# A chunked-attention and softplus-FFN kernel: the first product of six of its nine token tiles by Strassen's seven products

## The chip, the core and the metric

The kernel runs on one core of a Trainium2 chip. The core has a matrix engine (TensorE, in the profile PE, with its weight loads as PEld), a vector engine (VectorE, DVE), a scalar engine (ScalarE, ACT), GpSimd (POOL), a queue engine (SyncE, SP) and sixteen DMA engines. Each engine takes its instructions in the order of the program and waits on semaphores. The metric is the device time of one execution in microseconds; less is better. Three runs before the change took 861.62 to 861.96 us, with a median of 861.85 us.

## The reference

Attention within chunks of 64 tokens (8 batches, 8 heads, 576 tokens, head size 64), then a feed-forward layer with softplus on 4608 tokens, all in float32:

```python
scores = scale * np.matmul(q_c, k_c.transpose(0, 1, 2, 4, 3))
scores = scores - np.max(scores, axis=-1, keepdims=True)
attn = np.exp(scores)
attn = attn / (np.sum(attn, axis=-1, keepdims=True) + 1e-09)
x = np.matmul(attn, v_c)            # as 4608 x 512
h = x @ w_in                        # 512 x 2048
g = np.maximum(h, 0.0) + np.log1p(np.exp(-np.abs(h)))
out = g @ w_out                     # 2048 x 512
```

## The kernel before

**Tiles.** The 4608 tokens are nine m-tiles of 512 (`m`, four blocks of 128 tokens each, 36 blocks in all); the 2048 columns of `w_in` are 16 strips of 128 (`fc`). Each number is split into a high part rounded to `float32r` and the low rest, and each product is three matmuls: high by high, low by high, high by low. For one `m` and `fc` (number g = 16 m + fc) the first product G1 is 12 matmuls of 128x128 by 128x512 (four slices of K, three terms), from `gemm1` (L587). ACT then makes u = softplus (L595) and its high part `g_hi` (L599), DVE or POOL the low part `g_lo` (L603), and the second product G2 adds 12 matmuls (four tiles of 128 tokens, three terms, L621) into four PSUM banks `po`, which ACT and DVE evacuate (`ev`, L630) after the 16th strip. The tiles `g_hi` and `g_lo` have two buffers, u has one, and `pa`, PSUM for G1 and attention, has two tiles of two banks.

**Stages.** First some 30 us of attention for the first m-tile; then m-tile 0, beside which the weights are loaded and split ("decode", POOL and ACT, to about 120 us); then m-tiles 1 to 8, for which everything stands in SBUF.

**Attention** goes on beside the FFN in 17 *bursts* (`burst`, L462 and L550): a burst is the scores of one pair of blocks and the value product of the pair before. Around it ACT copies the result to x (L562) and does the exponentials (`exp`, L525, with a table load each way), DVE the maxima (L507), the subtraction (L512), the denominators (L530 to L532), the norm (L537) and transposes (L439, L474 and, for three blocks, L486); SP loads q, k, v in DMAs of 32 or 64 KB and swaps quarters of the transposed scores by DMA (`eT<-ka`).

**Order.** A planner (`class Plan`) is given every task with its engine, cost, needs, buffers and urgency, and its list schedule, made while the program is built, fixes the order of instructions on each engine; nothing is reordered at run time. The order of PE is given by the list `seq`: G1 of g, then G2 of g - 1, with bursts after given G1. DMAs of SP and ACT take eight semaphores in turn, so that a DMA also waits for the one eight places before it in the program, whichever of the two queues that is on.

Of the kernel before, what the change touches and what calls it, by code (L numbers as in the profile page):

```python
# [33 lines left out]
class Plan:  # L34
# [14 lines left out]
    def add(  # L49
        self, name, eng, cost, fn, needs=(), urg=0.0, table=None, take=(), kb=0, slack=0.0, after=(), port=False, parts=1,  # L50
        late={}
# [3 lines left out]
            take=take, kb=kb, slack=slack, seq=len(self.tasks), port=port or eng == "POOL", parts=parts, late=late,  # L55
        )

    def order(self):
# [23 lines left out]
        def has_room(t, now):  # L82
            for pool, _ in t["take"]:
                cap, used = self.pools[pool]
                if len(used) >= cap:
                    for n in used[len(used) - cap]:
                        if n not in fin or fin[n] + self.CROSS > now:
                            return False
            return True
# [59 lines left out]
def chunked_attention_softplus_ffn(  # L149
# [54 lines left out]
    wi = [tuple(const.tile([P, KC, half], F32R, name=n) for n in ("wi_hi", "wi_lo"))]  # L204
    stage = [later.tile([P, KC * half], F32, name="wib") for _ in range(2)]
# [4 lines left out]
    early = [xpool.tile([P, TPM, DM], F32, name="x") for _ in range(2)]  # L210
    xs = []

    def x_of(m):
        while len(xs) <= min(m, 1):
            xs.append([xpool.tile([P, 2 * TPM, KC, C], F32R, name="x") for _ in range(2)])
        return xs[m % 2]
# [6 lines left out]
    tops = [const.tile([P, UW], I32, name=f"top{j}") for j in range(TOP_BUFS)]  # L223
    for t in tops:
        nc.vector.memset(t, 0)
    live = {}

    def raw_tile():
        return ld.tile([P, 2 * UW + 16], I32, name="raw", bufs=RAW_BUFS)
# [4 lines left out]
    def w_load(u, is_in, fc):  # L234
        queue = nc.gpsimd if u in LOAD_POOL else nc.sync
        raw = raw_tile()
# [17 lines left out]
    def w_low(u):  # L254
        if u < STAGED:
            o = u * UW
            low = stage[o // (KC * half)][:, o % (KC * half) :][:, :UW].bitcast(I32)
        else:
            low = ld.tile([P, UW], I32, name="low", bufs=LOW_BUFS)
# [7 lines left out]

    def w_parts(u, is_in, fc):
        t = live["low", u].bitcast(F32)
        if is_in:  # L270
            if fc // HALF_FC == len(wi):
                wi.append(tuple(later.tile([P, KC, half], F32R, name="wib") for _ in range(2)))
# [655 lines left out]
```

## Time and profile before

| | before |
|---|---|
| median of three runs | 861.85 us |
| span of the profiled execution, first to last instruction | 859.1 us |
| PE busy | 847.1 us, 99% |
| DVE, ACT, POOL busy | 346.8, 314.0, 75.1 us |
| DMA | 63.13 MB, mean 73 GB/s |

The profile gives the profiled execution's own time as its span of 859.1 us; the median of the runs is 2.75 us above it, which lies before the first and after the last instruction. In the groups a row is line, engine, operation, tiles, count, then busy time and mean duration, then the idle time before it and what ended it. In a timeline a row is start (us), duration (us), engine, line, operation. "xN" is a count of instructions. Busy times of PE overlap a little: a 128x512 matmul is shown with 389 ns, while the next one starts earlier.

### The profile page before, as it was taken

The numbers are of one execution on the slowest core, as the hardware profiler recorded it, in microseconds if no ns is written. First come the engines' busy times: TensorE is split into PE (matmuls) and PEld (weight loads), VectorE is DVE, ScalarE is ACT, GpSimd is POOL, SyncE is SP. The second block draws the span as 40 slices with busy tenths as digits, with TensorE's granted clock in tenths as the row PEclk, the third lists the DMA queues.
The fourth block names the chain that finished last, engine by engine and source line by source line (L and its number), as shares of the span: only waits on it lengthen the run. The fifth ranks groups of instructions, "written<-read, shape, count | busy, mean of one in ns | idle before, by whom it ended". The sixth has DMA issues, their size and how long they took to land.

```text
span 859.1 us, 14819 instructions
## 1 busy us (share of the span) xinstructions
PE 847.1 (99%) x5889; PEld 700.6 (82%) x5889; DVE 346.8 (40%) x600; ACT 314.0 (37%) x493; POOL 75.1 (9%) x76
## 2 busy tenths in 40 slices
PE   8899999999999999999999999999999999999997
PEld 7687888888888888888888888888888888888886
DVE  4999865333433251515252333424342514121111
ACT  4857744322424242424242423324242324222222
POOL 1576751000000000000000000000000000000000
PEclk9999999999999999999999999999999999999999
DMA  9987733222232224232323223222312241010001
GB/s 225 237 213 188 222 92 94 47 46 50 43 98 42 50 43 102 41 58 36 87 54 60 39 53 96 42 52 41 98 41 53 42 103 37 13 50 0 1 1 49
DMA packets 207061, 63.13 MB, mean 73 GB/s; under 512 B 184592, under 2 KB 200464, under 8 KB 206992
## 3 DMA queue, kind: packets, MB, share of 16 engines
q1 hardware_dynamic: 206848, 62.06, 31.6%
q8 instruction: 46, 0.75, 0.4%
q14 instruction: 23, 0.19, 0.1%
q10 hardware_dynamic: 144, 0.13, 0.0%
HBM read 45.09 MB, written 9.44 MB: 63 GB/s over the span
## 4 chain that ended last, share of the span: by engine, by line
PE 90%; DVE 3%; DMA 2%; SPq 1%; ACT 1%; issue 1%; POOL 0%; DVEq 0%; POOLq 0%; ACTq 0%
PE po L621 43%; PE pa L587 42%; PE pa L550 2%; DMA raw<-in_moe_w_in_dram 2%; PE pa L462 2%; SPq L318 1%; DMA raw<-in_moe_w_out_dram 1%; DVE wib L266 1%; DVE qe L449 1%; DVE ka L449 1%; DVE g_lo L603 0%; DVE eT L486 0%; ACT u L595 0%; ACT wib L261 0%; ACT top L252 0%
## 5 line engine op out<-in xcount | busy, mean ns | idle before, releaser
L603 DVE TENSOR_TENSOR g_lo<-u,g_hi 128x512 fp32r<-128x512 f32 (+1 forms) x133 | 92.5, 696 | 441.8 <-ACT g_hi L599 441.6
L595 ACT ACTIVATE u<-pa 128x512 f32<-128x512 f32 (+1 forms) x146 | 86.4, 592 | 503.6 <-PE pa L587 496.3
L587 PE MATMUL pa<-x,wib 128*128 128x512 f32 x864 | 207.5, 389 | 0.0
L587 PEld LDWEIGHTS pa<-x,wib 128*128 128x128 f32 x864 | 162.2, 188 | 33.7
L587 PE MATMUL pa<-x,wi_hi 128*128 128x512 f32 (+1 forms) x592 | 186.1, 383 | 0.0
L621 PE MATMUL po<-late,g_hi 128*128 128x512 f32 x539 | 166.2, 391 | 0.1
L587 PEld LDWEIGHTS pa<-x,wi_hi 128*128 128x128 f32 x592 | 109.6, 188 | 22.0
L621 PEld LDWEIGHTS po<-late,g_hi 128*128 128x128 f32 x539 | 100.5, 188 | 21.6 <-POOL late L291 0.5
L621 PE MATMUL po<-wo_hi,g_hi 128*128 128x512 f32 x288 | 109.5, 393 | 0.0
L621 PE MATMUL po<-wo_lo,g_hi 128*128 128x512 f32 x288 | 108.7, 390 | 0.6 <-POOL wo_lo L291 0.6
L621 PE MATMUL po<-wo_hi,g_lo 128*128 128x512 f32 x288 | 108.7, 390 | 0.0
L587 PE MATMUL pa<-x,wi_lo 128*128 128x512 f32 (+1 forms) x296 | 108.6, 383 | 0.0
L621 PE MATMUL po<-late,g_lo 128*128 128x512 f32 x287 | 107.8, 389 | 0.0
L599 ACT CAST g_hi<-u 128x512 fp32r<-128x512 f32 (+1 forms) x146 | 89.7, 615 | 4.4
L621 PEld LDWEIGHTS po<-wo_lo,g_hi 128*128 128x128 f32 x288 | 54.0, 188 | 12.1 <-POOL wo_lo L291 1.0
L587 PEld LDWEIGHTS pa<-x,wi_lo 128*128 128x128 f32 x296 | 54.7, 188 | 10.9
L621 PEld LDWEIGHTS po<-wo_hi,g_lo 128*128 128x128 f32 x288 | 54.0, 188 | 11.5 <-DVE g_lo L603 0.3
L621 PEld LDWEIGHTS po<-late,g_lo 128*128 128x128 f32 x287 | 53.9, 188 | 11.3
L621 PEld LDWEIGHTS po<-wo_hi,g_hi 128*128 128x128 f32 x288 | 53.7, 188 | 11.2
L530 DVE TENSOR_REDUCE den<-qe 128x8 f32<-128x512 f32 x32 | 21.1, 661 | 23.2 <-ACT qe L525 23.2
L566 DVE TENSOR_TENSOR x<-pa,x 128x512 fp32r<-128x512 f32 x36 | 24.5, 682 | 1.8 <-ACT x L562 1.8
L439 DVE STREAM_TRANSPOSE ka<-k 128x512 f32<-128x512 f32 x28 | 19.8, 706 | 13.3 <-DMA eT<-ka 13.3
(114 smaller groups left out, 581.9 us busy)
## 6 DMA issues: line engine op xcount, KB each, us to landing
out_dram<-raw SPq DMA_DIRECT2D x35, 256.0 KB, 2.4
raw<-in_moe_w_in_dram SPq DMA_DIRECT2D x16, 512.0 KB, 5.2
raw<-in_moe_w_out_dram SPq DMA_DIRECT2D x16, 512.0 KB, 4.6
eT<-ka SPq DMA_DIRECT2D x232, 32.0 KB, 1.9
q<-in_q_dram SPq DMA_DIRECT2D x224, 32.0 KB, 2.1
k<-in_k_dram SPq DMA_DIRECT2D x224, 32.0 KB, 2.1
q<-in_v_dram SPq DMA_DIRECT2D x60, 64.0 KB, 2.4
k<-in_v_dram SPq DMA_DIRECT2D x60, 64.0 KB, 2.4
```

What stands on the lines that cost most here:

```text
L266: nc.vector.tensor_tensor(low, low, live.pop(("top", u)), op=ALU.add)
L439: nc.vector.transpose(t, live.pop((n, i)))
L449: nc.vector.transpose(dst[d : d + BL, :, tb], src[s : s + BL, :, dh])
L462: nc.tensor.matmul(pa[o, c2, col : col + C], qT[r, a * HP + hl, :], kT[r, a * HP + hl, :], start=True, stop=True,)
L530: nc.vector.tensor_reduce(den, e, axis=AX.X, op=ALU.add)
L550: nc.tensor.matmul(pa[o, a, col : col + C], vt[r, 4 * j + 2 * h2 + c2, :], eT[r, :, 4 * c2 + 2 * j + h2, :], start=True, stop=True,)
L566: nc.vector.tensor_tensor(lo, live.pop(("xp", i)), hi.bitcast(F32), op=ALU.subtract)
L587: nc.tensor.matmul(ph, wt[:, c, fs], x[:, ts_, c, :], start=(n == 0), stop=(n == 3 * KC - 1))
L595: nc.scalar.activation(w["u"], w["ph"], AF.Softplus)
L599: nc.scalar.copy(w["hi"], w["u"])
L603: (nc.gpsimd if pool else nc.vector).tensor_tensor(w["lo"], w["u"], w["hi"].bitcast(F32), op=ALU.subtract)
L621: nc.tensor.matmul(pos[w["m"]][t], terms[n][0][:, j * P : (j + 1) * P], terms[n][1], start=(w["first"] and n == 0), stop=n == 2 and (w["la ...
```

## The change

**What it does.** `FAST = 3`: m-tiles 0 to 2 stay as they are. M-tiles 3 to 8 are taken in three *supers* of two m-tiles (1024 tokens). Within a super, two strips `fc` at a time (a *pair*, eight per super), the product of 2x2 blocks (two m-tiles; two strips; two halves of K) is formed by seven products P0 to P6 instead of eight. Each product is six matmuls (two slices of K, three terms), so a pair has 42 where it had 48; there are 24 pairs. P4, P5, P6 accumulate on the banks of P1, P2, P0, after ACT has copied what these held (`hold`: s0, s1, s2); POOL (`d`, `e`) and DVE (`c22`, `f`, `f2`, `c11`) then combine them (`mix`).

**Weight sums.** The seven weight operands of each pair are formed once during m-tiles 1 and 2 (`w_total`, `w_sums`, `w_sum_lo` on POOL: per pair two operations of 128x512, five of 128x256, then two of 128x512 and one of 128x256; `w_sum_hi` and the stores on ACT: 48 stores of sums and 12 of unchanged blocks), and written to DRAM (`scratch`, 1.75 MB a pair). In each super the operands of each pair come back in two loads on ACT's queue (`ring_load`: 1 MB for P0 to P3, free after P3 of the pair before; 0.75 MB for P4 to P6, free after P6).

**Sums of x.** Before each super five sums of blocks of x (`x_sum`, k = 2 and 4 on POOL), and seven splits into high (`x_hi`, ACT) and low (`x_lo`, DVE), all 128x1024.

**Half of u in DRAM.** The pairs yield u for both m-tiles; that of the second goes to DRAM (`spill_store`, 512 KB a pair) and comes back (`spill_load`) in the super's second phase, in which the 16 G2 of the second m-tile follow one another without a G1. In the first phase PE does P0 to P6 of a pair (six matmuls each), then the two G2 of the pair before.

**Attention.** Bursts move: nine of the seventeen stand in m-tiles 0 to 2 (after G1 4, 8, 15, 21, 26, 31, 35, 40, 44), four each in supers 0 and 1 (after pairs 2, 5, 7 and after the ninth G2 of the second phase). From block 9 on the swaps by DMA become DVE transposes (eight of 32x256 per block), and the norms of blocks 10 to 19 go to POOL.

The core of the diff:

```diff
-    later = ctx.enter_context(tc.tile_pool(name="later", bufs=2))
+    FAST = 3
+    HC = MT // 2
+
+    later = ctx.enter_context(tc.tile_pool(name="later", bufs=4))
     late = ctx.enter_context(tc.tile_pool(name="late", bufs=LATE))
     const = ctx.enter_context(tc.tile_pool(name="const", bufs=1))
-    xpool = ctx.enter_context(tc.tile_pool(name="xpool", bufs=4))
+    xpool = ctx.enter_context(tc.tile_pool(name="xpool", bufs=2))
+    dram = ctx.enter_context(tc.tile_pool(name="dram", bufs=1, space=bass.MemoryType.DRAM))
...
+    def high(n):
+        if "high" not in live:
+            live["high"] = [later.tile([P, 4 * MT], F32R if j < 3 else F32, name="wib") for j in (0, 1, 2, 3)]
+        return live["high"][n]
+
+    def x_image(k):
+        if k < NX:
+            return [t.rearrange("p a k f -> p (a k f)")[:, 2 * MT * k : 2 * MT * (k + 1)] for t in wi[0]]
+        return high(k - NX)[:, : 2 * MT], high(k - NX)[:, 2 * MT :]
...
+    def w_image(w, k):
+        if w["name"] == "0_0" and k < NX:
+            return raw_tile(1 + k // 2).bitcast(F32R)[:, k % 2 * MT : (k % 2 + 1) * MT]
+        t = x_of(FAST - 1)[k // NX].rearrange("p s k t -> p (s k t)")
+        return t[:, k % NX * MT : (k % NX + 1) * MT]
...
+    def w_total(j, n):
+        if n == 0:
+            live["wt", j] = raw_tile(0)
+        hi, lo = (w.bitcast(F32) for w in wi_of(2 * j + n))
+        dst = live["wt", j][:, n * UW : (n + 1) * UW].rearrange("p (k f) -> p k f", k=KC)
+        nc.gpsimd.tensor_tensor(dst, hi, lo, op=ALU.add)
+
+    def w_sum_parts(j):
+        wt = live["wt", j]
+        s, h = top_all.bitcast(F32), low_all.bitcast(F32)
+        return [(s[:, :MT], h[:, :MT]), (s[:, MT:], h[:, MT:]), (wt[:, HC : 2 * HC], wt[:, :HC])]
+
+    def w_sums(j, n):
+        (s0, _), (s1, _), (s2, _) = w_sum_parts(j)
+        t = [live["wt", j][:, i * HC : (i + 1) * HC] for i in range(4)]
+        out, a, b, op = (
+            (s0[:, :HC], t[0], t[3], ALU.add), (s0[:, HC:], t[2], t[3], ALU.add), (s1[:, :HC], t[2], t[0], ALU.subtract),
+            (s1[:, HC:], t[0], t[1], ALU.add), (s2, t[1], t[3], ALU.subtract),
+        )[n]
+        nc.gpsimd.tensor_tensor(out, a, b, op=op)
+
+    def w_sum_hi(j, n):
+        s, h = w_sum_parts(j)[n]
+        nc.scalar.copy(h.bitcast(F32R), s)
+
+    def w_sum_lo(j, n):
+        s, h = w_sum_parts(j)[n]
+        nc.gpsimd.tensor_tensor(s, s, h, op=ALU.subtract)
...
+    def w_own_store(b, q, i):
+        src = wi[b][q].bitcast(F32)[:, i::2, 2 * i : 2 * i + 2, :].rearrange("p a k f -> p a (k f)")
+        to = scratch[(0, 4, 6)[b] : (4, 6, 8)[b]]
+        to = to.rearrange("a p (n q c) -> p a n q c", n=7, q=2)[:, :, 2 + 2 * i, q]
+        nc.scalar.dma_start(to, src)
+    def ring_load(w, part):
+        src = scratch[w["j"]]
+        if w["name"] == "0_0" and part == 0:
+            for n in range(2):
+                nc.scalar.dma_start(raw_tile(1 + n, True), src[:, 2 * n * MT : 2 * (n + 1) * MT])
+            return
+        t = x_of(FAST - 1)[part].rearrange("p s k t -> p (s k t)").bitcast(F32)
+        cols = slice(NX * MT, 7 * MT) if part else slice(0, NX * MT)
+        nc.scalar.dma_start(t[:, : cols.stop - cols.start], src[:, cols])
...
+    def x_sum(n, k):
+        a, b = (x_block(*ij) for ij in OF_X[k])
+        eng = nc.gpsimd if k in XS_POOL else nc.vector
+        eng.tensor_tensor(x_sum_of(n, k), a, b, op=X_SUMS[k])
...
+    def x_hi(n, k):
+        hi, _ = x_image(k)
+        nc.scalar.copy(split(hi), x_of_product(n, k))
+
+    def x_lo(n, k):
+        hi, lo = (split(t) for t in x_image(k))
+        eng = nc.gpsimd if k in XL_POOL else nc.vector
+        eng.tensor_tensor(lo, x_of_product(n, k), hi.bitcast(F32), op=ALU.subtract)
+
+    def product(w, k):
+        if "bank" not in w:
+            w["bank"] = [t[:, n] for t in (pa_tile(), pa_tile()) for n in range(2)]
+        wts = w_image(w, k).rearrange("p (q k f) -> p q k f", q=2, k=2)
+        hi, lo = (t.rearrange("p (k c) -> p k c", k=2) for t in x_image(k))
+        for c in range(2):
+            for n, (q, x) in enumerate(((0, hi), (1, hi), (0, lo))):
+                nc.tensor.matmul(
+                    w["bank"][BANK[k]], wts[:, q, c, :], x[:, c, :], start=k < NX and c + n == 0, stop=c == 1 and n == 2,
+                    skip_group_check=True,
+                )
+
+    def hold(w, n):
+        nc.scalar.copy(tmp_of(n), w["bank"][n])
+
+    def mix(w, what):
+        s1, s2, s3, f = (tmp_of(n) for n in range(4))
+        x, y, z, v = w["bank"]
+        out, a, b, op = {
+            "d": (s2, s3, s2, ALU.subtract),
+            "e": (s1, s1, s2, ALU.add),
+            "c22": (s1, s1, v, ALU.add),
+            "f": (f, y, s2, ALU.add),
+            "f2": (f, f, z, ALU.subtract),
+            "c11": (f, f, x, ALU.add),
+        }[what]
+        (nc.gpsimd if what in MIX_POOL else nc.vector).tensor_tensor(out, a, b, op=op)
...
+    def soft(w, i, j):
+        src = {(0, 0): tmp_of(3), (0, 1): w["bank"][2], (1, 0): w["bank"][1], (1, 1): tmp_of(0)}[i, j]
+        nc.scalar.activation(u_tiles(j)[i], src, AF.Softplus)
+        if j == 0:
+            w["first"][i]["u"] = u_tiles(0)[i]
+
+    def spill_store(w):
+        nc.scalar.dma_start(spill[w["s"]][w["j"]], top_all.bitcast(F32))
+
+    def spill_load(w):
+        nc.scalar.dma_start((top_all, low_all)[w["j"] % 2].bitcast(F32), spill[w["s"]][w["j"]])
+        for i in range(2):
+            w["second"][i]["u"] = u_tiles(1 - w["j"] % 2)[i]
...
-    SWAP_DVE = (4,7,9)
+    SWAP_DVE = (4,7) + tuple(range(9, 36))
...
-    NORM_POOL = (0,2,3,4,5,6,7)
-    GLO_POOL = (0,2,4,5,6,8,9,10,12,15,16,17,19)
+    NORM_POOL = (0,2,3,4,5,6,7) + tuple(range(10, 20))
+    GLO_POOL = (0,2,4,5,6,8,9,10,12,15)
...
-    BURST_AT = (6, 14)
+    BURST_AT = (21, 26, 31, 35, 40, 44)
+    IN_SUPER = ((0, 2), (0, 5), (0, 7), (1, 8))
+    XS_POOL = (2, 4)
+    XL_POOL = ()
+    MIX_POOL = ("d", "e")
+    PM = 1.36
...
+
+    behind = plain[-1:]
+    for n in range(len(SUPERS)):
+        mine = pairs[n * FC // 2 : (n + 1) * FC // 2]
+        for w in mine:
+            seq += [f"P{k}_{w['name']}" for k in range(7)]
+            seq.append(f"G2_{behind[0]['name']}")
+            add_burst(n, 0, w["j"])
+            seq += [f"G2_{v_['name']}" for v_ in behind[1:]]
+            behind = w["first"][::-1]
+        seq += [f"G2_{v_['name']}" for v_ in behind]
+        second = [v_ for w in mine for v_ in w["second"]]
+        last = n == len(SUPERS) - 1
+        for v_ in second if last else second[:-2]:
+            seq.append(f"G2_{v_['name']}")
+            add_burst(n, 1, v_["fc"])
+        behind = second[-2:]
...
+            take = []
+            if k == 0:
+                take = [("pa", [f"c11_{name}", f"soft10_{name}"]), ("pa", [f"soft01_{name}", f"c22_{name}", f"f2_{name}"])]
+            plan.add(f"P{k}_{name}", "PE", PM, partial(product, w, k), needs, urg=1e6, take=take)
```

**What moves, on PE.** Before, the end of one G1 (L587; 12 matmuls) and the start of the G2 (L621) behind it:

```order
L587 MATMUL pa<-x,wi_hi 128x512 x2
L587 MATMUL pa<-x,wi_lo 128x512
L587 MATMUL pa<-x,wi_hi 128x512
L621 MATMUL po_2524<-wo_hi,g_hi 128x512
L621 MATMUL po_2524<-wo_lo,g_hi 128x512
```

After, in the first super, the end of a pair's products (L763, of which the last row is P4 to P6) and the start of a G2 (L818):

```order
L763 MATMUL pa<-wi_hi,xb 128x512 x2
L763 MATMUL pa<-wi_lo,xb 128x512
L763 MATMUL pa<-wib,xb 128x512 x18
L818 MATMUL po_3959<-late,g_hi 128x512 x2
L818 MATMUL po_3959<-late,g_lo 128x512
```

A G1 stands between two G2 no longer; 42 matmuls come in one piece, then 24.

**What moves, on ACT, where the second phase of super 0 begins.** Before, the order at any burst (u and g_hi as above; L562 is x, `qe` the exponentials, L525):

```order
L595 ACTIVATE u<-pa 128x512
L599 CAST g_hi<-u 128x512
L562 CAST x<-pa 128x4x2x64 x2
L595 ACTIVATE u<-pa 128x512
L599 CAST g_hi<-u 128x512
L525 ACT_TABLE_LOAD
L525 ACTIVATE qe<-qe 128x512 x2
L595 ACT_TABLE_LOAD
L595 ACTIVATE u<-pa 128x512
L599 CAST g_hi<-u 128x512
```

After, from the last burst of the first phase (L643 is g_hi, L608 x, L724 a ring load, L798 a load of spilled u, L825 the evacuation of `po`, L570 the exponentials; the last row is g_hi of the first two G2 of the second m-tile):

```order
L643 CAST g_hi<-low 128x512
L608 COPY xa<-pa 128x4x2x64
L724 DMA xb<-scratch 128x1536
L608 COPY xa<-pa 128x4x2x64
L643 CAST g_hi<-low 128x512
L798 DMA top<-spill_109 128x1024
L798 DMA low<-spill_109 128x1024
L825 COPY raw_5002<-po_3959 128x512
L825 COPY raw_5008<-po_3961 128x512
L570 ACT_TABLE_LOAD
L570 ACTIVATE qe<-qe 128x512
L643 CAST g_hi<-top 128x512 x2
```

The evacuations, a table load and an exponential now stand ahead of the g_hi that the next G2 needs; before, that G2 had a G1 ahead of it.

**What moves, on ACT and DVE, at the last burst of super 0.** ACT after (L749 is `x_hi`; `low`, `top` hold the reloaded u):

```order
L608 COPY xa<-pa 128x4x2x64 x2
L643 CAST g_hi<-low 128x512
L749 CAST wib<-xa 128x1024
L643 CAST g_hi<-low 128x512
L749 CAST wi_hi<-wib 128x1024
L749 CAST wi_hi<-raw_4981 128x1024
L749 CAST wi_hi<-xa 128x1024
L749 CAST wib<-wib 128x1024
L570 ACTIVATE qe<-qe 128x512 x2
L643 CAST g_hi<-top 128x512
L798 DMA low<-spill_109 128x1024
L643 CAST g_hi<-top 128x512
```

DVE before, at a burst (L566 is the low part of x):

```order
L603 TENSOR_TENSOR g_lo<-u,g_hi 128x512 x2
L566 TENSOR_TENSOR x<-pa,x 128x4x2x64
L507 TENSOR_REDUCE mx<-pa 128x8
L512 TENSOR_TENSOR qe<-pa,mx 128x512
L507 TENSOR_REDUCE mx<-pa 128x8
L566 TENSOR_TENSOR x<-pa,x 128x4x2x64
L512 TENSOR_TENSOR qe<-pa,mx 128x512
L603 TENSOR_TENSOR g_lo<-u,g_hi 128x512
L530 TENSOR_REDUCE den<-qe 128x8
L531 TENSOR_SCALAR den<-den 128x8
```

DVE after, at that place (L552, L557 maxima and subtraction; L742 `x_sum`; L754 `x_lo`):

```order
L552 TENSOR_REDUCE mx<-pa 128x8
L742 TENSOR_TENSOR raw_4981<-xa 128x1024
L557 TENSOR_TENSOR qe<-pa,mx 128x512
L552 TENSOR_REDUCE mx<-pa 128x8
L647 TENSOR_TENSOR g_lo<-low,g_hi 128x512
L557 TENSOR_TENSOR qe<-pa,mx 128x512
L647 TENSOR_TENSOR g_lo<-low,g_hi 128x512
L754 TENSOR_TENSOR wi_lo<-raw_4981,wi_hi 128x1024
L754 TENSOR_TENSOR wi_lo<-xa,wi_hi 128x1024
L647 TENSOR_TENSOR g_lo<-top,g_hi 128x512
L754 TENSOR_TENSOR wi_lo<-wib,wi_hi 128x1024
L742 TENSOR_TENSOR xa<-xa 128x2x8x64
```

Operations of 128x1024 on x, for the next super, now stand among the g_hi and g_lo of a run of G2.

More of the change, by code (lines that the diff above doesn't have):

```diff
@@ L203, in chunked_attention_softplus_ffn @@
     sp.tile([P, G_PAD], F32, name="pad", bufs=1)
-    wi = [tuple(const.tile([P, KC, half], F32R, name=n) for n in ("wi_hi", "wi_lo"))]
-    stage = [later.tile([P, KC * half], F32, name="wib") for _ in range(2)]
+    wi = [tuple(const.tile([P, HALF_FC, KC, P], F32R, name=n) for n in ("wi_hi", "wi_lo"))]
+    stage = [later.tile([P, 4 * MT], F32, name="wib") for _ in range(4)]
     wo_hi = const.tile([P, HALF_FC, DM], F32R, name="wo_hi")
@@ L876, in chunked_attention_softplus_ffn @@
                  [before[f"G2_{name}"], f"lo{name}", f"w_lo{of_out[fc]}", f"w_hi{of_out[fc]}"], urg=1e6, take=take,
-                 after=["T1"] if w["first"] and name == "a0" else ["E3"] if m == 0 and w["first"] else [], late=slow)
+                 after=["T1"] if w["first"] and name == "a0" else ["E3"] if m == 0 and w["first"] else [], late=slow, room=room)
         if w["last"]:
```

375 lines of the change are left out of this document (295 added, 80 removed).

## The prediction

> **What bounds the kernel now.** I read the page first: busy shares, then the chain that ended last.
>
> ```profile
> span 859.1 us, 14819 instructions
> PE 847.1 (99%) x5889; PEld 700.6 (82%) x5889; DVE 346.8 (40%) x600; ACT 314.0 (37%) x493; POOL 75.1 (9%) x76
> ...
> PE 90%; DVE 3%; DMA 2%; SPq 1%; ACT 1%; issue 1%; POOL 0%; DVEq 0%; POOLq 0%; ACTq 0%
> PE po L621 43%; PE pa L587 42%; PE pa L550 2%; DMA raw<-in_moe_w_in_dram 2%; PE pa L462 2%; SPq L318 1%; DMA raw<-in_moe_w_out_dram 1%; DVE wib L266 1%; DVE qe L449 1%; DVE ka L449 1%; DVE g_lo L603 0%; DVE eT L486 0%; ACT u L595 0%; ACT wib L261 0%; ACT top L252 0%
> ```
>
> PE is busy 99% of the span, and G1 and G2 (L587, L621) are 85% of the chain. The same by stage, from the windows (columns: window, length, then busy time and count of PE, PEld, DVE, ACT, POOL, the clock, the share of DMA time, GB/s):
>
> ```profile
> 64.00:107.00 43.00, 42.36 (x305) 34.99 (x304) 39.51 (x68) 32.96 (x53) 29.51 (x27) 1.00 0.74 202
> 107.00:120.00 13.00, 12.88 (x112) 10.21 (x114) 10.91 (x19) 7.38 (x13) 8.25 (x10) 1.00 0.43 126
> 120.00:200.00 80.00, 80.00 (x547) 66.36 (x539) 32.17 (x59) 26.94 (x42) 6.42 (x5) 1.00 0.30 62
> 300.00:400.00 100.00, 100.00 (x679) 82.84 (x678) 37.08 (x65) 33.87 (x52) 0.00 (x0) 1.00 0.28 58
> ```
>
> From 120 us on PE has no hole and the others are busy two fifths of the time, so a matmul that goes shortens the kernel by its pitch until some other engine makes PE wait. The pitch is in the chain by time, and the price of a burst in ACT's timeline (softplus after G1, with and without a burst between):
>
> ```profile
> 186.25 2.72 PE pa L587 x12
> 188.97 2.72 PE po L621 x12
> ```
>
> ```profile
> 199.89 0.60 ACT L595 ACTIVATE u<-pa 128x512 f32<-128x512 f32 x1 [4.19 <-PE pa L587]
> 205.32 0.60 ACT L595 ACTIVATE u<-pa 128x512 f32<-128x512 f32 x1 [4.19 <-PE pa L587]
> ...
> 213.04 0.60 ACT L595 ACTIVATE u<-pa 128x512 f32<-128x512 f32 x1 [5.07 <-PE pa L587]
> ...
> 214.31 1.28 ACT L525 ACT_TABLE_LOAD   x1
> 215.60 1.15 ACT L525 ACTIVATE qe<-qe 128x512 f32<-128x512 f32 x2
> ```
>
> Twelve matmuls take 2.72 us, 0.2267 us each. A round of G1 and G2 takes 5.44 us, with a burst 7.72, so a burst costs 2.28.
>
> **The matmuls removed.** 24 pairs times 6 are 144 matmuls: -32.64 us. The 17 bursts remain 17. A pair is now 7 x 1.36 = 9.52 us of products and two G2, 5.44. Decode up to the 20th round keeps its order on all engines, so the first 120 us stay.
>
> **The ring of weights.** The 1 MB load for P0 to P3 may start when P3 of the pair before ends and must land before the next P0: P4 to P6 and two G2 later, 4.08 + 5.44 = 9.52 us. The 0.75 MB load has 5.44 + 5.44 = 10.88. No DMA of before has this size, so I bound it (issues: count, KB each, median us to landing; then a row of GB/s in 40 slices of 85 to 125 us; then SP's queue issuing one DMA, min/median/max ns):
>
> ```profile
> out_dram<-raw SPq DMA_DIRECT2D x35, 256.0 KB, 2.4
> raw<-in_moe_w_out_dram SPq DMA_DIRECT2D x16, 512.0 KB, 4.6
> q<-in_q_dram SPq DMA_DIRECT2D x224, 32.0 KB, 2.1
> ...
> GB/s 391 381 412 290 126 28 68 299 295 320 153 80 53 34 48 184 365 259 315 312 269 327 362 205 16 76 114 109 250 238 39 92 111 20 0 31 49 34 63 68
> ...
> L637 SPq DMA_DIRECT2D out_dram<-raw x35: 332/430/1281, 130.7 to 854.9; - x35
> ```
>
> The slow bound goes on from 256 to 512 KB (2.2 us for 256 KB more): 9.0 us, with 0.43 of issue 9.4, just in time. The fast bound takes 391 GB/s: 2.7 us for 1 MB plus the 1.7 that 2.4 leaves beside 256 KB, 4.4. I take 5, nearer the fast one, since the 512 KB loads shared the engines with each other: no wait, 0 us. Spilled u (512 KB) is read a G2 pair ahead, 4.6 within 10.88 for two buffers: 0.
>
> **Beside the pair.** P4 needs s1 2.72 us after P1 ended; a copy from PSUM on ACT is 0.58 (below). The next P0 needs `c11`, one DVE operation, with 2.72 us or more of G2 over it. Softplus, four per pair as before, `hold` and `mix` with three DMA issues add some 3 us of ACT, 2.7 of DVE and 2.6 of POOL to 14.96 us, in which ACT and DVE have had about two fifths: hidden.
>
> **The second phase.** Here a G2 follows a G2, g_hi has two buffers, so ACT may begin g_hi of one when the G2 two before ends, and the next G2 starts 2.72 us later; its low part is first read two matmuls in, at 3.17. Groups by form, and for 1024 columns the step from 256 to 512, taken twice more:
>
> ```profile
> L603 DVE TENSOR_TENSOR g_lo<-u,g_hi 128x512 fp32r<-128x512 f32 x130 | 90.8, 699 | 441.7 <-ACT g_hi L599 441.6
> L599 ACT CAST g_hi<-u 128x512 fp32r<-128x512 f32 x142 | 88.1, 621 | 4.3
> L630 DVE COPY raw<-po 128x512 f32<-128x512 f32 x17 | 11.0, 678 | 2.3 <-PE po L621 2.1
> L630 ACT COPY raw<-po 128x512 f32<-128x512 f32 x18 | 10.4, 584 | 5.0 <-PE po L621 5.0
> L291 POOL TENSOR_TENSOR wib<-low,wib 128x512 fp32r<-128x512 f32 x6 | 7.8, 1294 | 0.2
> ...
> L599 ACT CAST g_hi<-u 128x256 fp32r<-128x256 f32 x4 | 1.6, 400 | 0.1
> ...
> L603 POOL TENSOR_TENSOR g_lo<-u,g_hi 128x256 fp32r<-128x256 f32 x1 | 0.7, 737 | 0.0
> L651 DVE COPY raw<-po 128x256 f32<-128x256 f32 x1 | 0.4, 425 | 1.1 <-ACT raw L651 1.1
> ```
>
> So 1024 columns: ACT 1.06, DVE 1.18, POOL 2.41. Undisturbed, 0.62 + 0.70 fit into 3.17 with some 1.6 us to spare: 0. Three places are disturbed.
>
> Start of super 0's second phase, counted from the end of its burst: three G2 run to 8.16, the last of them m-tile 3's. ACT must evacuate its banks (ready at 6.3 and 7.7, done 8.3), then does the table load (1.28) and one exponential (0.6) to 10.2, and only then g_hi, to 10.85. PE waits from 8.16 to 10.9, then 0.3 for g_lo: **+3.0**. In super 1 the exponentials stand ahead of the evacuations and cost nothing, but DVE evacuates the fourth bank (ready at 8.4) before g_lo, done 9.8 against 8.6: **+1.2**. Super 2 has no burst: 0.
>
> Last burst of super 0, counted from its end: POOL sums x until 3.3 and 5.7; ACT does five `x_hi` and two exponentials (to 8.8) ahead of the g_hi that the G2 of 8.16 needs, and DVE does maximum, `x_sum`, subtraction and maximum (to 3.3) ahead of a g_lo needed at 3.17. If nothing else waits, that is 0.9 + 0.8 + 0.4 = 2.1. But DVE and POOL wait for each other, as here (timeline):
>
> ```profile
> 62.49 1.28 POOL L603 TENSOR_TENSOR g_lo<-u,g_hi 128x512 fp32r<-128x512 f32 x1
> 62.55 1.76 DVE L291 TENSOR_TENSOR wi_lo<-wib,wi_hi 128x512 fp32r<-128x512 f32 x1 [0.51 <-POOL wi_hi L287]
> 77.33 0.68 DVE L291 TENSOR_TENSOR wib<-low,wib 128x512 fp32r<-128x512 f32 x1
> ```
>
> The DVE operation that began in a POOL operation took 1.76 us, the one alone 0.68. With `x_sum` on DVE behind POOL's (2.41), g_lo comes near 7.5 instead of 4: 4.4 in all. I take **+4.0**; ends 2.1 and 4.4. Super 1 to 2 has no exponentials and another order: **+0.5**, ends 0 and 2.
>
> [...]
>
> **The weight sums, rounds 17 to 47.** POOL's 8 x (2.6 + 3.7 + 3.3) = 77 us and ACT's 13 us of casts and 60 issues at 0.43 (26 us) lie in 175 us. PE feels them only if a burst comes late, or if g_hi does, 3.3 us of cover. Two gaps between bursts are four rounds, 21.76 us. The work between bursts, as in this one before (DVE timeline):
>
> ```profile
> 120.95 0.69 DVE L566 TENSOR_TENSOR x<-pa,x 128x512 fp32r<-128x512 f32 x1 [1.76 <-ACT x L562]
> ...
> 124.08 0.68 DVE L512 TENSOR_TENSOR qe<-pa,mx 128x512 f32<-128x512 f32 x1
> 130.20 0.69 DVE L530 TENSOR_REDUCE den<-qe 128x8 f32<-128x512 f32 x1 [5.44 <-ACT qe L525]
> 130.92 0.17 DVE L531 TENSOR_SCALAR den<-den 128x8 f32<-128x8 f32 x1
> 131.13 0.20 DVE L532 RECIPROCAL den<-den 128x8 f32<-128x8 f32 x1
> ...
> 135.83 3.54 DVE L486 STREAM_TRANSPOSE eT<-qe 32x256 f32<-32x256 f32 x8
> ```
>
> is 3.8 (to the subtraction's end) + 2.4 (table, two exponentials) + 1.1 + 1.3 (norm, on POOL) + 7.1 (two blocks of transposes, where one went by DMA) + 2.1 (transposes of the next q and k) + 2.8 (four g_lo) = 20.6, so 1.2 us to spare. Each g_lo that meets POOL adds up to 1.1, each norm that waits behind a weight sum 1.3: up to 7, 5.8 late, twice 11.6. Nearest is the decode stage (64 to 107: POOL 69% busy, PE waiting 0.64 of 43 us). I take **+3**; ends 0 and 11.6.
>
> **Sum.** -32.64 + 3.0 + 1.2 + 4.0 + 0.5 + 3.0 = -20.9: the span goes from 859.1 to 838.2. The median of the runs, 861.85, is 2.75 above the span, which I keep: **841 us**. Under 0.2%, 1.7 us, a measurement of this kernel can't tell from no change.
>
> **The rivals.**
> *Cover holds everywhere:* the planner's order leaves no holes and only the matmuls count: 829.2, to 833 with one hole of 4. For it: 100.00 busy in 100 us. Against: the g_hi behind table load and evacuation can't come sooner in that order. 0.15.
> *Bursts come late:* the chain of 20.6 us meets POOL at every turn, 11.6 instead of 3, and holes of 0.5 in half of the second-phase G2 of supers 0 and 1 (16 x 0.5 = 8): 858, from 851 on. 0.15.
> *Loads wait for loads (slower):* each DMA waits for the one eight before it, on either queue. If a ring load stands behind eight q loads just planned, these are issued and landed in
>
> ```profile
> 119.83 4.52 SPq L432 DMA_DIRECT2D q<-in_q_dram  x8
> ```
>
> 4.5 + 2.1 = 6.6 us, and the ring load lands 6.6 + 5 = 11.6 after P3: 2.1 late. In all 16 pairs of supers 0 and 1 that is 34 us: 875. It decides from 1.3 us late per pair. Against: only some 40 small DMAs belong to a burst, and most were issued long before. 0.08.
> My forecast, 834 to 851, has 0.60; 0.02 is left for no change.
>
> **Range.** From the first rival's lower part to the second's: 830 to 856; under it I leave 0.07, above it 0.12. Faster by more than 0.2%: 0.90; within: 0.02; slower: 0.08.
>
> **What would show it.** In the profile after, PE's busy time falls by about 32 to 815 us, and its holes, 12 us before, grow to some 24, in four or five places: g_hi (L643) after the last burst of super 0's first phase, 3 us; g_lo there in super 1; g_lo and g_hi around the `x_hi` before super 1; a few at bursts after G1 35 and 44. P0 waiting for a `scratch` load would make me wrong towards slower, and waits of g_lo all over the second phase; no waits there, towards 829. If PE's clock falls below 1.00 in the holes, the sum is too low.

## The result, and the profile after

The changed kernel takes **884.31 us** (median of four runs, 882.7 to 886.54), the kernel before 861.74 in the same job: ratio 1.0263, 95% interval 1.0248 to 1.0279. It is slower by 22.6 us, where 841 had been forecast. (In this execution time and span differ by 1.8 us; of the 2.75 set beside the kernel before, only about that much lies outside the span, and the rest is that its profiled execution was shorter than the median.) The page of the profiled execution (884.0 us, span 882.2):

```profile
span 882.2 us, 15154 instructions
PE 834.6 (95%) x5745; PEld 676.0 (77%) x5745; DVE 521.4 (59%) x876; ACT 388.8 (44%) x614; POOL 242.0 (27%) x217
...
PEclk9999999999989999999999999999999999999999
...
PE 66%; DVE 11%; DMA 8%; ACT 4%; issue 4%; POOL 3%; SPq 3%; ACTq 0%; DVEq 0%; POOLq 0%
```

PE has 144 matmuls less, but it is now idle for 47.6 us instead of 12, and it is 66% of the chain instead of 90%; DVE, DMA, ACT, POOL and SP's queue hold the rest. The time can be put to two places. The softplus after G1 of round 46 is the same step in both kernels, and up to it the new kernel has only three more bursts. ACT's timeline at that step, before and after:

```profile
296.91 0.60 ACT L595 ACTIVATE u<-pa 128x512 f32<-128x512 f32 x1 [4.19 <-PE pa L587]
```

```profile
329.56 0.60 ACT L639 ACTIVATE u<-pa 128x512 f32<-128x512 f32 x1
```

Three bursts of 2.28 would bring 296.91 to 303.75; it is 329.56. So **25.8 us are lost up to round 46** (0.4 of them before round 14), the rounds in which the weight sums are made. From there to the end the kernel before takes 562.2; less 32.64 and less the three bursts that is 522.7; the new one takes 552.6, so **29.9 us are lost in the supers**. 25.8 + 29.9 - 32.64 is the 23.1 by which the span grew.

**The first place.** The windows from 200 to 310 us (before: PE 110.00 busy, clock 1.00):

```profile
200.00:310.00 110.00, 99.25 (x759) 80.17 (x758) 66.17 (x124) 43.62 (x68) 54.83 (x56) 0.94 0.49 118
```

PE waits 10.75 us there, and its granted clock is 0.94 on average. The chain by time shows one of the stalls whole:

```profile
244.27 0.04 ACT u L639
244.31 0.04 issue
244.35 2.15 DMA scratch<-top
246.53 0.31 SPq L477
...
247.87 0.45 SPq L477
...
251.46 0.53 DMA xa<-in_k_dram
...
254.65 0.72 DVE ka L484
255.37 0.04 issue
255.42 1.13 PE pa L507 x32
256.55 5.30 PE po L818 x12
```

Read downwards: ACT starts a softplus, then issues the store of a weight sum that stood behind it; SP's queue, in the middle of its loads of q and about to load k, goes on only when that store has landed (DMAs of SP and ACT take eight semaphores in turn); then come the loads, DVE's transpose of k, and PE. Before the chain closes, the timelines of DVE and of ACT show the other half:

```profile
250.34 0.71 DVE L484 STREAM_TRANSPOSE qe<-xa 128x512 f32<-128x512 f32 x1 [5.54 <-DMA xa<-in_k_dram]
250.98 1.01 DVE L647 TENSOR_TENSOR g_lo<-u,g_hi 128x512 fp32r<-128x512 f32 x1
```

```profile
244.27 0.60 ACT L639 ACTIVATE u<-pa 128x512 f32<-128x512 f32 x1 [4.84 <-DVE g_lo L647]
...
252.08 0.60 ACT L639 ACTIVATE u<-pa 128x512 f32<-128x512 f32 x1 [6.55 <-DVE g_lo L647]
```

DVE waits 5.54 us for the loads, and g_lo stands behind in its order; ACT's next softplus waits 6.55 us for that g_lo, because u has one buffer. The softplus at 244.27 had waited 4.84 us in the same way, and the store right behind it is the one that SP waited for. It is a circle: ACT holds SP, SP holds DVE, DVE holds ACT.

**The second place.** The chain in super 2, one pair:

```profile
752.50 6.81 PE pa L763 x30
759.31 0.02 issue
759.33 0.61 ACT low L790
...
760.03 0.70 DVE wib L782
760.74 0.04 issue
760.78 1.66 PE pa L763 x6
762.44 5.44 PE po L818 x24
```

After five products (P0 to P4) the chain leaves PE, which does P5 meanwhile: ACT reads P4's bank (`low`), then DVE reads it (`wib`), and only then the last product, P6, runs, though that writes another bank, the other half of the same tile. A pair takes 15.38 instead of 14.96 here, and more in supers 0 and 1, where ACT and DVE have other work. PE's waits from 330 us to the end:

```profile
PE pa L763 <- DVE wib L782: 9.4, 8, 1.6
PE po L818 <- DVE g_lo L647: 4.8, 5, 2.0
PE pa L763 <- ACT low L790: 2.7, 4, 0.7
PE po L818 <- ACT g_hi L643: 2.5, 1, 2.5
```

### The profile page after: what moved, and what is told of

It is laid out like the page before. It is cut to its first block, busy times and chain, and to the rows that moved or that the text cites. A ratio compares the mean times of both kernels' runs of the same rounds, so it can differ in the third digit from the quotient of the medians.

```text
span 882.2 us, 15154 instructions
## 1 busy us (share of the span) xinstructions
PE 834.6 (95%) x5745; PEld 676.0 (77%) x5745; DVE 521.4 (59%) x876; ACT 388.8 (44%) x614; POOL 242.0 (27%) x217
## 4 chain that ended last, share of the span: by engine, by line
PE 66%; DVE 11%; DMA 8%; ACT 4%; issue 4%; POOL 3%; SPq 3%; ACTq 0%; DVEq 0%; POOLq 0%
PE po L818 36%; PE pa L763 20%; PE pa L631 7%; DVE wib L782 2%; DVE g_lo L647 2%; DVE eT L531 2%; SPq L477 2%; DMA raw<-in_moe_w_out_dram 2%; PE pa L595 1%; DMA q<-in_q_dram 1%; ACT low L790 1%; SPq L349 1%; PE pa L507 1%; DMA raw<-in_moe_w_in_dram 1%; POOL wib L782 1%
## 5 line engine op out<-in xcount | busy, mean ns | idle before, releaser
L818 PE MATMUL po<-late,g_hi 128*128 128x512 f32 x539 | 168.0, 395 | 0.1
L782 POOL TENSOR_TENSOR wib<-wib 128x512 f32<-128x512 f32 x48 | 62.6, 1304 | 333.3 <-ACT wib L769 331.4
L763 PE MATMUL pa<-wib,xb 128*128 128x512 f32 x432 | 109.0, 397 | 13.5 <-DVE wib L782 9.4
L818 PE MATMUL po<-wo_hi,g_lo 128*128 128x512 f32 x288 | 111.7, 400 | 9.6 <-DVE g_lo L647 9.6
L818 PEld LDWEIGHTS po<-late,g_hi 128*128 128x128 f32 x539 | 101.1, 189 | 22.0 <-POOL late L322 0.6
L818 PE MATMUL po<-wo_hi,g_hi 128*128 128x512 f32 x288 | 111.7, 400 | 2.5 <-ACT g_hi L643 2.5
L818 PE MATMUL po<-late,g_lo 128*128 128x512 f32 x287 | 109.1, 394 | 4.4 <-DVE g_lo L647 4.4
L763 PE MATMUL pa<-wi_hi,xb 128*128 128x512 f32 x368 | 113.3, 389 | 0.0
L818 PE MATMUL po<-wo_lo,g_hi 128*128 128x512 f32 x288 | 110.8, 397 | 0.6 <-POOL wo_lo L322 0.6
L763 PEld LDWEIGHTS pa<-wib,xb 128*128 128x128 f32 x432 | 79.2, 188 | 39.3 <-DVE wib L782 19.2
L531 DVE STREAM_TRANSPOSE eT<-qe 32x256 f32<-32x256 f32 x232 | 100.5, 433 | 8.2 <-POOL qe L582 4.9
L647 DVE TENSOR_TENSOR g_lo<-low,g_hi 128x512 fp32r<-128x512 f32 x72 | 54.4, 757 | 73.1 <-ACT g_hi L643 72.6
L643 ACT CAST g_hi<-low 128x512 fp32r<-128x512 f32 x72 | 44.7, 621 | 87.8 <-PE po L818 84.9
L763 PEld LDWEIGHTS pa<-wi_hi,xb 128*128 128x128 f32 x368 | 69.1, 188 | 14.3
L818 PEld LDWEIGHTS po<-wo_hi,g_lo 128*128 128x128 f32 x288 | 55.2, 192 | 24.9 <-DVE g_lo L647 13.4
L639 ACT ACTIVATE u<-pa 128x512 f32<-128x512 f32 (+1 forms) x50 | 29.1, 581 | 97.8 <-PE pa L631 52.7
L763 PE MATMUL pa<-wi_lo,xb 128*128 128x512 f32 x184 | 71.6, 389 | 0.0
L818 PEld LDWEIGHTS po<-late,g_lo 128*128 128x128 f32 x287 | 54.3, 189 | 18.0 <-DVE g_lo L647 6.6
L818 PEld LDWEIGHTS po<-wo_hi,g_hi 128*128 128x128 f32 x288 | 54.8, 192 | 14.7 <-ACT g_hi L643 3.2
L782 DVE TENSOR_TENSOR wib<-wib,pa 128x512 f32<-128x512 f32 x72 | 49.1, 687 | 27.9 <-ACT top L790 14.7
L818 PEld LDWEIGHTS po<-wo_lo,g_hi 128*128 128x128 f32 x288 | 55.1, 192 | 12.7 <-POOL wo_lo L322 1.1
```

Source lines behind the costliest of these rows:

```text
L531: nc.vector.transpose(live["eT", i][d : d + BL, tb], e[s : s + BL, kb])
L639: nc.scalar.activation(w["u"], w["ph"], AF.Softplus)
L643: nc.scalar.copy(w["hi"], w["u"])
L647: (nc.gpsimd if pool else nc.vector).tensor_tensor(w["lo"], w["u"], w["hi"].bitcast(F32), op=ALU.subtract)
L763: nc.tensor.matmul(w["bank"][BANK[k]], wts[:, q, c, :], x[:, c, :], start=k < NX and c + n == 0, stop=c == 1 and n == 2, skip_group_check= ...
L782: (nc.gpsimd if what in MIX_POOL else nc.vector).tensor_tensor(out, a, b, op=op)
```

## The experiments

Each row gives the time, the ratio to the kernel before with its interval, the softplus of round 46 and the time from there to the end of the span (both of the profiled execution). The last four rows are tried on top of banks and stores on POOL's queue. The kernels without sums or stores, and the one that stores ready data, don't form the weights that the pairs need; they only measure time.

| run | time | ratio | round 46 | rest |
|---|---|---|---|---|
| changed kernel | 884.3 | 1.0263 (1.0248-1.0279) | 329.6 | 552.6 |
| banks in turn | 864.8 | 1.0041 (1.0021-1.0060) | 328.3 | 534.7 |
| no stores | 867.0 | 1.0058 (1.0038-1.0078) | 313.5 | 552.7 |
| no sums, no stores | 866.4 | 1.0051 (1.0031-1.0071) | 311.0 | 553.0 |
| stores on POOL's queue | 871.8 | 1.0115 (1.0100-1.0130) | 317.4 | 551.6 |
| stores of ready data | 879.8 | 1.0213 (1.0196-1.0231) | 322.9 | 553.8 |
| banks, casts and stores later | 883.2 | 1.0253 (1.0233-1.0273) | 325.8 | 555.3 |
| banks, no sums | 851.5 | 0.9882 (0.9865-0.9899) | 313.5 | 534.9 |
| banks, stores on POOL's queue | **854.3** | **0.9925 (0.9907-0.9943)** | 322.7 | 533.3 |
| ... and norms on DVE | 855.1 | 0.9934 (0.9915-0.9954) | 316.5 | 535.6 |
| ... and block 8's swap on DVE | 860.5 | 0.9991 (0.9978-1.0004) | 321.8 | 534.0 |
| ... and six bursts moved | 859.7 | 0.9974 (0.9962-0.9986) | 319.8 | 542.0 |
| ... and one burst moved | 856.9 | 0.9949 (0.9935-0.9963) | 319.0 | 535.0 |

The profiled execution of banks with stores on POOL's queue was one of its longer ones, 857.8, and reached round 14 3.7 us later than the changed kernel. The column "round 46" is one execution each, and it scatters: the two kernels without sums have the same decode stage but for the banks, and show 311.0 and 313.5. Differences of 2 or 3 us in it say little.

**Banks in turn.**

```diff
-            w["bank"] = [t[:, n] for t in (pa_tile(), pa_tile()) for n in range(2)]
+            ta, tb = pa_tile(), pa_tile(); w["bank"] = [ta[:, 0], tb[:, 0], ta[:, 1], tb[:, 1]]
-                take = [("pa", [f"c11_{name}", f"soft10_{name}"]), ("pa", [f"soft01_{name}", f"c22_{name}", f"f2_{name}"])]
+                take = [("pa", [f"c11_{name}", f"soft01_{name}", f"f2_{name}"]), ("pa", [f"soft10_{name}", f"c22_{name}", f"f_{name}"])]
```

> The changed kernel with its seven products' four PSUM banks dealt out in turn to the two PSUM tiles (first, third in one, second, fourth in the other), so that no product writes into the tile that the copy of the product before is reading. Theory (a copy or an addition on one half of a tile waits for a product into the other half): PE's waits for `wib` (9.4 us) and `low` (2.7 us) in front of the products go, the stretch from the softplus of round 46 to the end falls from 552.6 us to about 541, and the time from 884 to about 872. Rival (the chain hold, d, e, c22 is itself too long beside a pair, whatever the banks): the waits only move, less than 3 us, 881 or more.

It took 864.8, which is 19.5 us less. Of the 19.2 by which the span is shorter, 17.9 lie after round 46 (534.7 against 552.6), 6 more than the theory's 11.6. The chain in super 2 is now what the prediction had written for a pair, 9.52 and 5.44, and of PE's waits those before a product are all but gone:

```profile
735.43 9.52 PE pa L763 x42
744.95 5.44 PE po L818 x24
750.39 9.52 PE pa L763 x42
```

```profile
PE po L818 <- DVE g_lo L647: 4.8, 5, 2.0
PE po L818 <- ACT g_hi L643: 2.4, 1, 2.4
PE pa L763 <- ACT wib L769: 0.9, 4, 0.2
PE pa L507 <- DVE ka L484: 0.6, 2, 0.4
```

From the first copy of a super's first pair to that of its last (seven pairs) the changed kernel takes 113.0, 116.8 and 109.3 us, this one 107.7, 110.3 and 104.7: 16.3 us in the pairs. The waits that the profile names were 12.1; the rest fits what a product loses when it starts anew (six matmuls in 1.66 against 1.36 us), but was not measured by itself. Two halves of one PSUM tile are one thing to the dependencies of this program: a product into one half waits for who reads the other, and a reader waits for the product into the other. The copy of P0's bank shows the second: in the pair above it starts 2.75 us after the pair (755.25), behind P1, and with the banks in turn 1.40 us after it (736.83), behind P0.

**No stores; no sums; stores on POOL's queue.** In the first two 50 of the 60 stores (all but the first pair's sums and four of unchanged blocks), and then the sums of the other seven pairs too, are left out, and all pairs read the first pair's weights.

```diff
-                plan.add(..., partial(w_sum_store, j, n, q), ...)
+                plan.add(..., partial(w_sum_store, j, n, q) if j == 0 else lambda: None, ...)
-                plan.add(..., partial(w_own_store, b, q, i), ...)
+                plan.add(..., partial(w_own_store, b, q, i) if b == 0 else lambda: None, ...)
-        src = scratch[w["j"]]
+        src = scratch[0]
```

> The changed kernel with the weight sums of the first pair alone stored (10 of the 60 stores; all pairs read the first pair's weights); all sums are still computed, and the order of all other instructions is kept. In the changed kernel the softplus of round 46 starts at 329.6 us; with the three bursts that were moved ahead of it and nothing lost it would be 303.7. Theory (loads of q, k and v on SP wait, through the eight semaphores that SP's and ACT's DMAs share, for stores that wait for POOL): round 46 at 309 or before, time about 864. First rival (the sums themselves: POOL's share of DVE's time, and norms that wait in POOL's order): round 46 at 322 or later, 877 or more. Second rival (the bursts stand too close for their own chain): 322 or later too.

> As the kernel without the 50 stores, and the sums of the other seven pairs left out as well (their POOL operations and ACT casts). Theory (shared semaphores): within 3 us of the kernel without stores, round 46 at 306 to 309. First rival (the sums themselves): round 46 at 305 to 309 only here, 322 or later there. Second rival (the bursts' own chain): still 320 or later.

```diff
-        nc.scalar.dma_start(to[:, at, q], src.rearrange("p (n c) -> p n c", c=HC))
+        nc.gpsimd.dma_start(to[:, at, q], src.rearrange("p (n c) -> p n c", c=HC))
-        nc.scalar.dma_start(to, src)
+        nc.gpsimd.dma_start(to, src)
```

> The changed kernel with all 60 stores of weight sums issued from POOL's queue instead of ACT's; its DMAs use semaphores of their own, so SP's loads no longer wait for them. Theory (shared semaphores): round 46 at 309 to 315, time 864 to 870; what an issue costs on POOL no run here shows yet, at 1 us each it would be 60 us of POOL in some 190, and POOL has some 90 to spare. Rivals (the sums themselves, or the bursts' own chain): round 46 at 325 or later, 880 or more.

Round 46 comes 16.1 us sooner without the stores, though every sum is still computed, 2.5 more without the sums, and 12.2 sooner with all stores and sums in place but another queue. So the sums by themselves cost little (2.5 us here, 0.6 by the medians, neither clear of the scatter); what costs is the stores in ACT's queue. The 313.5 is later than the 309 expected, and 317.4 later than 315; some 7 us remain when sums and stores are gone (311.0 against 303.75). SP's queue, eight loads in a group, in the changed kernel and with the stores on POOL's queue:

```profile
240.10 7.72 SPq L477 DMA_DIRECT2D xa<-in_q_dram  x8
247.87 5.01 SPq L477 DMA_DIRECT2D xa<-in_k_dram  x8
```

```profile
236.38 4.43 SPq L477 DMA_DIRECT2D xa<-in_q_dram  x8
240.86 3.94 SPq L477 DMA_DIRECT2D xa<-in_k_dram  x8
```

The stores themselves are no cheaper there. Rows of the line of the stores, first in ACT's queue, then in POOL's (ns, minimum, median, maximum of an issue):

```profile
L708 ACTq DMA_DIRECT2D scratch<-top x16: 366/366/576, 135.9 to 304.8; - x16
```

```profile
L708 POOL DMA_DIRECT2D scratch<-top x16: 725/725/748, 137.8 to 295.5; - x16
```

An issue takes twice as long (725 ns against 366 in these rows) and still the kernel is 12.5 us faster. The edit changes three things at once: the semaphores, what stands in ACT's order, and the kind of the queue (the page lists POOL's as `q0 software_dynamic`). The first shows by itself in SP's queue, in its waits from 120 to 330 us of the changed kernel:

```profile
SPq L477 <- DMA scratch<-low: 16.0, 7, 6.8
SPq L477 <- DMA scratch<-top: 4.6, 4, 2.7
SPq L477 <- DMA scratch<-raw: 4.3, 3, 2.4
```

With two smaller rows these waits for stores come to 27.8 us, though none of the loads reads what a store writes. Over the same stretch they are 2.1 us without the 50 stores, and none with the stores on POOL's queue. So not only ACT's time for the issues went with this edit, but SP's waits for the stores as well, because this program ties SP's and ACT's DMAs together through shared semaphores. How the 12.5 us divide between the two was not measured.

**Stores of ready data; casts and stores later.** What makes a store late: the sum on POOL, or ACT's order?

```diff
-        src = w_sum_parts(j)[n][1 - q]
+        src = wi[0][q].bitcast(F32)[:, 0].rearrange("p k f -> p (k f)")[:, : (MT, MT, HC)[n]]
```

> The changed kernel, its order kept, but the 48 stores of sums write a slice of `wi_hi` or `wi_lo`, long decoded, instead of the sum, so that none of them waits for POOL or for ACT's cast (the sums are still computed, and what the pairs read for five of the seven products is not the sum). If SP's loads are late because the stores wait for POOL's sums: round 46 at 312 to 318, as without stores. If they are late because the stores stand in ACT's order behind a softplus that itself waits (for u, which waits for g_lo, which stands on DVE behind transposes that wait for the loads: a circle through ACT, SP and DVE): round 46 at 324 or later, as in the changed kernel at 329.6.

```diff
-            plan.add(f"wh{j}_{n}", "ACT", ..., urg=d + W_URG)
+            plan.add(f"wh{j}_{n}", "ACT", ..., urg=d + W_URG, slack=4.0)
-                plan.add(f"wd{j}_{n}{q}", "ACT", ..., kb=190 * part)
+                plan.add(f"wd{j}_{n}{q}", "ACT", ..., kb=190 * part, slack=5.0)
```

> Banks in turn; the stores stay on ACT's queue with the shared semaphores, but the planner places the ACT cast of a sum 4 us and its store 5 us later than it holds the data ready (a slack on either), so that what they wait for is done when their turn comes. Theory (a store that waits for POOL in ACT's order holds up ACT and, through the semaphore, SP's loads): round 46 at 312 to 320, time 848 to 857. Rival (the mere number of DMAs on the shared semaphores and ACT's 0.43 us for each issue): round 46 at 326 or later, 862 or more.

With ready data round 46 comes at 322.9, between the two expectations: 6.7 of the 16.1 us are waits for the sums (4.5 by the medians), the other 9.4 come with stores whose data lay ready, and for which SP still waits at least 19.8 us (9.2 + 5.5 + 3.3 + 1.8 in its four largest rows of such waits). That leaves ACT's order, the circle of the first section, and the issues as such, which were not told apart. The slack missed its expectation: 325.8, only 2.5 sooner than with the banks alone (328.3), and the time rose to 883.2, 18.4 more than with the banks alone. The last store of a sum is issued at 337.0 us, where the changed kernel issues it at 306.4. Behind it the split `wi_hi`, for which the first product waits, starts at 347.63, after a wait of 12.70 us that the profile puts down to a load of q. PE's waits of that kernel, from 330 to 440 us:

```profile
PE pa L763 <- ACT wi_hi L749: 14.8, 1, 14.8
```

Placing a store later in the same queue didn't free what waits behind it. The expectations did not foresee that loss.

**Both edits together, and the floor.**

> Both edits at once: the products' banks dealt out in turn to the two PSUM tiles, and the 60 stores of weight sums on POOL's queue. If the two losses lie in different stages and have causes of their own, the gains add: round 46 at 317 as with the stores on POOL's queue, 535 from there to the end as with the banks alone, so 852 to 855, below the 862.0 of before. If one of them only covered the other: 860 or more.

> Banks in turn, and the weight sums and stores of all pairs but the first left out (all pairs read the first pair's weights; 10 stores remain). It gives the floor that a cheaper way of making the sums could reach with this order of bursts: round 46 at 311, 535 after it, 846 to 849. If the shorter decode stage brings new collisions into the supers: 852 or more.

The gains add: 854.3, **0.75% faster than the kernel before** (0.57% to 0.93%). Without the sums of seven pairs it is 851.5, 2.5 above the range expected; round 46 comes at 313.5 there, not 311. So with this order of bursts the weight sums and their stores still cost some 3 us, and the forecast of 841 stays 10 us below even a kernel that doesn't make them. The page of both edits:

```profile
span 856.0 us, 15155 instructions
PE 824.2 (96%) x5745; PEld 675.1 (79%) x5745; DVE 527.1 (62%) x876; ACT 389.8 (46%) x614; POOL 283.7 (33%) x277
```

**Four tries to go on.** On top of both edits: norms on DVE, block 8's swap on DVE, and bursts moved (the last in two forms; two buffers that wait for the burst after round 35 then wait for the one after 36).

```diff
-    NORM_POOL = (0,2,3,4,5,6,7) + tuple(range(10, 20))
+    NORM_POOL = (0,2,3,4,5,6,7)
```

> Banks in turn, stores on POOL's queue, and the normalisations of blocks 10 to 19 moved from POOL to DVE. If norms that wait in POOL's order behind weight sums still hold up the bursts (DVE's transposes waited 8.7 us for them with the stores on POOL's queue), 2 to 4 us less than banks and stores alone: 849 to 852. If DVE, which gets ten more operations of 0.7 us, is the tighter engine: the same or up to 2 us more.

```diff
-    SWAP_DVE = (4,7) + tuple(range(9, 36))
+    SWAP_DVE = (4,) + tuple(range(7, 36))
```

> Banks in turn and stores on POOL's queue, and block 8's swap of halves by DVE transposes instead of eight DMAs on SP. The hole of 3 us between the softplus of rounds 18 and 19 was there with and without the sums, and behind it stands a transpose that waits 4.15 us for those eight DMAs: if it goes, 851 to 852 instead of 854; if DVE's 3.5 us of transposes bring a hole of the same size in its place, 854 again.

```diff
-    BURST_AT = (21, 26, 31, 35, 40, 44)
+    BURST_AT = (20, 25, 31, 36, 41, 45)
```

> Banks in turn and stores on POOL's queue, and the six bursts of the decode stage after rounds 20, 25, 31, 36, 41 and 45 instead of 21, 26, 31, 35, 40 and 44, so that five rounds stand behind the burst of 31 instead of four. If the bursts' own chain (some 20 us against four rounds of 5.44) makes the holes of 3 us around rounds 32 and 36: 850 to 852 instead of 854. If the holes belong to the collisions with the sums and not to the spacing: 853 to 856.

```diff
-    BURST_AT = (21, 26, 31, 35, 40, 44)
+    BURST_AT = (21, 26, 31, 36, 40, 44)
```

> Banks in turn, stores on POOL's queue, and one burst moved by one round (after rounds 21, 26, 31, 36, 40 and 44 instead of 35 in the fourth place). With all six bursts moved, rounds 31 to 41 ran with a hole less, but the burst moved to 20 brought a wait of 5.2 us at its start. If the spacing counts burst by burst, this one keeps the gain and not the loss: 850 to 853 instead of 854. If every move only shifts the holes: 853 to 860.

None gained. The norms make no difference (855.1), as was expected if DVE is the tighter engine. The swap on DVE costs 6 us and the six moved bursts 5, more than either of their expectations allowed: with the burst after round 20, PE waits 5.2 us once for u, and the stretch behind round 46 takes 542.0. (The profiled execution was the longest of twelve, 863.6 against a median of 859.7, with the clock at 0.98 from 330 to 520 and from 650 to 720 us; why was not found.) The gain that was looked for is there: from round 31 to 36, with one burst, 29.5 us, which is five times 5.44 and 2.28, where both edits alone take 38.1 with two bursts, 6.3 above that measure. It is lost again elsewhere. One burst moved gives 856.9, in the middle of what was expected if holes only shift, and its interval overlaps that of both edits alone. In these four tries a step taken from one place came back as a delay elsewhere; which of the remaining waits could be had without another was not found.

## Why the prediction was wrong

The span was forecast at 838.2 and is 882.2, 44.0 more: 22.8 of it up to round 46 (25.8 lost where 3 was forecast) and 21.2 in the supers (29.9 where 8.7 was forecast).

**The weight sums, +3 (ends 0 and 11.6): mis-sized, 25.8.** This is the step that failed first. The prediction priced what the sums do to DVE and to the norms by the operations between two bursts; without the sums round 46 came only 2.5 us sooner, so that part was not too low. It counted ACT's 26 us of issues as time on an engine with room, and did not ask what stands behind those stores. 16.1 us hang on the stores: some 6.7 on waits for the sums and some 9.4 on the rest. About 7 us remained with sums and 50 stores out; the first pair's stores, the spacing of the bursts and the clock were not told apart.

**"Beside the pair ... hidden", 0: it was 16.3.** The durations were right (copy 0.59, addition 0.69, on POOL 1.30), and the cover was counted for P4 and for the next P0. What was left out is what P6 waits for: the readers of the other half of its tile. The edit that deals out the banks in turn brought the pair to the 14.96 of the prediction.

**The rival "loads wait for loads" named the right link in the wrong place.** It had the eight shared semaphores, and a DMA waiting for the one eight before it on the other queue. But it put the loss into the ring loads of supers 0 and 1. There no product waits for `scratch`, and the ring loads land as forecast, 5.4 us for 1 MB where 5 was taken:

```profile
xb<-scratch ACTq DMA_DIRECT2D x23, 1024.0 KB, 5.4
xb<-scratch ACTq DMA_DIRECT2D x24, 768.0 KB, 5.1
```

The link acted while the weight sums were made, on the loads of q, k and v, where ACT's DMAs wait for something themselves. That this rival's 875 lies nearest to the measured time is chance.

**The second phase, 8.7: the total near, two of its parts not.** From the first copy of a super's last pair to that of the next super's first lie seven products (9.52), 18 G2 (48.96) and two bursts (4.56), 63.0 us. Super 0 to 1 took 70.9, 7.8 lost where 3.0 + 4.0 was forecast (70.1 with the banks in turn). Super 1 to 2 took 67.2, 4.2 lost where 1.2 + 0.5 was forecast. At the start of the phase the terms fit: PE waits 2.54 us for g_hi and 0.32 for g_lo at 476 us (3.0 forecast), and 0.93 and 0.25 for g_lo at 663 and 669 us (1.2 forecast). After the last burst they don't: there is one wait for g_lo of 1.36 at 510 us where 4.0 was forecast, and one of 1.99 at 697 us where 0.5 was. In super 0 the clock, at 0.50 from 477 to 480 us, made up for part of the difference; the sum had no term for it. So that the total came near is partly luck. (0.62 + 0.70 leave 1.85 of 3.17, not 1.6; the term stays 0.)

**The matmuls, -32.64: right.** With the waits gone, seven products take 9.52 us.

**The clock.** The prediction said that holes at a lower clock would make the sum too low. They did, but it is the smaller part. In the windows the granted clock is 0.94 from 200 to 310 us, which is worth at most some 6.6 us (an estimate: 0.06 of 110) of the 25.8. From 330 us to the end it is 1.00 on average, so it explains little of the 29.9. PE busy was 834.6, not 815, with the 144 matmuls fewer that were forecast.

## What to carry to other kernels

Ask of every DMA that a change adds not only what it costs to issue, but what it waits for in its queue, which semaphores it shares, and who is queued behind it: a store that nobody reads until the next stage can still hold up a load that somebody reads at once (here SP's loads waited 27.8 us for such stores). Put two accumulators that are read at different times into different tiles where dependencies are kept by the tile (16.3 us in the pairs here). And where a change takes DVE from 40% to 59% busy with single buffers between the engines, expect new waits: here a sum of terms read from the undisturbed kernel proved to be a floor and not an estimate.

## What the runs showed of the hardware

The granted clock fell to 0.50 at a burst whose longest wait was 2.10 us. PE's timeline around the stall shown above, in the changed kernel:

```profile
252.73 0.69 PE L595 MATMUL pa<-eT,xa 64*64 64x64 f32 x32 [2.10 <-ACT u L639]
255.42 1.13 PE L507 MATMUL pa<-ka,qe 64*64 64x64 f32 x32 [1.99 <-DVE ka L484]
256.48 0.79 PE L818 MATMUL po<-wo_hi,g_hi 128*128 128x512 f32 x1
257.07 0.63 PE L818 MATMUL po<-wo_lo,g_hi 128*128 128x512 f32 x1
257.50 0.63 PE L818 MATMUL po<-wo_hi,g_lo 128*128 128x512 f32 x1
```

From 257.1 to 261.3 us matmuls start 0.43 us apart instead of 0.227; these twelve take 5.30 us in the chain above instead of 2.72. Ahead of them stand two waits of 2.10 and 1.99 us, with 32 small 64x64 matmuls between the two, 64 before the first and 32 behind the second. The granted clock is 1.00 up to 254 us and 0.50 from 255 to 261.

The longest wait did not decide it here. A single wait of 2.76 us for g_lo, from 144.06 us on and with 128x512 matmuls on both sides, left the clock at 1.00; at a burst from 219.5 to 224.1 us two waits of 1.21 and 0.91 us were followed by a clock of 0.50 from 225 to 227 us. So the burst above cost 2.58 us (5.30 less 2.72) beyond its two waits of 4.09 together; whether the second wait or the small matmuls did it was not told apart.
